# Attention, MLP and routed experts on one core: weights decoded through PSUM, page lists read early, one branch at the end

## The chip, the cores and the metric

The kernel runs on one core of a Trainium2 chip. The metric is the device time of one execution in microseconds: for the kernel before, the median of three runs is 1185.52 us (1181.2 to 1187.52). A core has five instruction queues that run side by side and wait for one another through semaphores: TensorE (matmuls and transposes), VectorE, ScalarE, GpSimd and SyncE, which only starts DMA transfers here.

## What is computed

Three stages, each the input of the next, all in fp32:

```python
# attention: 4 batches x 8 heads x 768 tokens x 64; the first 4 tokens and a window of 128 are visible
scores = np.where(is_sink | in_window, q @ k.T / 8, -1e9)
a = np.exp(scores - scores.max(-1)); a = a / (a.sum(-1) + 1e-09)
x = merge_heads(a @ v)                        # 3072 tokens x 512
# MLP1: 512 -> 2048 -> 512
h = x @ w_in;  x = (h - np.tanh(h)) @ w_out
# routed experts, one of 8 per token: 512 -> 1024 -> 512
logits = x @ w_gate + modality_bias[modality_id]
e = argmax(logits);  out[e == i] = gate * (relu(x[e == i] @ w1[i]) @ w2[i])
```

## The kernel before

**Tiling and stages.** The 3072 tokens are 12 chunks of 256. A chunk has 8 attention units (one head each, 96 in all, numbered U) and one pass through MLP1: 16 blocks f of the hidden width, each with 12 matmuls of the first layer (`L1`, line 175) and 6 of the second (`L2`, line 245). After a chunk, its tokens are routed: VectorE works out a slot for each token, and GpSimd scatters the tokens' numbers and gates to a table `xs` in DRAM (line 653). When all chunks are through, 13 expert pages of 256 tokens follow (functions `m_*`): SyncE loads the number of the page from `order`, reads the page's list `mpl` out of `xs` (line 740), VectorE turns it into two index lists (`mi`, `ms`), GpSimd gathers the tokens' rows with them (`mx`, line 750), and TensorE runs the expert's two layers. The expert's weights are loaded as `mr` (line 723) and split into a high part `mh` on ScalarE and a low part `ml` on VectorE. GpSimd scatters the results to `out` (line 801).

**fp32 on TensorE.** Most products are made from such high and low parts, three matmuls for one. A split is a cast (line 208 on ScalarE, 210 on VectorE) and a subtraction (line 213, on GpSimd or VectorE); both are helpers, so many tiles share these lines. The first 14 units (`nf=14`) are not split ("plain" units).

**An attention unit.** Scores `s` into PSUM (`a_S`); VectorE masks them and takes the row minimum (lines 316, 323); ScalarE takes the exponential and the row sum (line 325); GpSimd and VectorE make the reciprocal (328, 329); `a_norm` multiplies the 128x160 tile by it on GpSimd (line 334); TensorE transposes the result (`a_T`); GpSimd applies triangular masks (352); `a_PV` multiplies by v into the PSUM tile R, which ScalarE copies out for plain units.

**Weights of MLP1.** Each of the 32 blocks (16 of w_in, 16 of w_out, 512 KB) arrives as 8-byte numbers, two 32-bit words each. `w_decode` makes an fp32 number of the two words with three VectorE operations (lines 144, 146, 148) on the SBUF tile y, then ScalarE casts the high part and GpSimd subtracts. This happens once, beside the first chunk.

**PSUM.** `ps(kind, ...)` hands out banks: two each for three groups, r (scores and transposes), h (first layer) and R (R, and the transposes `x`). A group's tiles take its two banks in turn, so the third waits until the first has been read. Two more banks collect the second layer.

**Order.** `run_chunks` writes each step as an event with a due time from a table of numbers, sorts the events and emits them; a scheduler then sets the order of each engine's instructions, which are run strictly in that order. Slots for the first three pages (`EARLY`) are settled by `r_order(False)` before the last chunk is routed, so that their work can begin beside it. `r_redo` makes a flag that says whether the input needs a general version of the first stages; it is loaded by each engine and branched on (lines 940, 941). Another branch (lines 910, 915) runs further pages where more than 13 are needed. Neither is taken with these inputs. Line 998 is the end of the program.

Of the kernel before, what the change touches and what calls it, by code (L numbers as in the profile page):

```python
# [27 lines left out]
PG = 256  # L28
NPG = NT // PG + NE - 1
PADID = 4096.0  # L30
EARLY = 3
NSTAT = NT // PG + 1
# [8 lines left out]
class Kern:  # L41
    def __init__(self, tc, a):
        self.tc, self.nc, self.a = tc, tc.nc, a
        self.Wi, self.Wo = {}, {}
        self.o = dict(tc='a', xa='g', mt0=-0.28, gz='v', mxe=11, lx='v', nf=14, efh='a', trc=-14.17, tpf=-1.86, xhi='v', vhi='a', vlo='g', qhi='a', khi='v', sT='a', tr='a', ev='a', glo='g', whi='a', wlo='g', gk=0, wl=-8.54, wls=1.25, wd=-3.86, wds=1.05, wo=1, bs=2, be=3, bE=3, bV=1, bg=2, btr=1, bxt=1, pt={'h': 'h', 's': 'r', 'T': 'r', 'R': 'R', 'x': 'R', 'Q': 'R'}, pb=(('r', 2), ('h', 2), ('R', 2)), tl=-9.97, ts=-5.86, tv=-4.34, tsv=-2.34, tS=-5.24, dS=0.07, tN=-4, dN=0.5, tT=-1.78, dT=0.35, tPV=-0.39, txs=-0.28, tg=0.64, tre=0.05, trl=0.48, trr=3.39, u0=-15.64, g=2, lag=3.4, raw=2, sp=2, ghi='a', qlo='g', klo='v', eh='v', xlo='v', x2=4, me=13, mxl=8.77, mxt=1.5, mlag=1.45, mwl=9.99, mws=3.27, mm=0, ev0='v', ghi0='a', vhi0='a', sT0='a', qhi0='a', xlo0='g', eh0='v', y=2)

# [91 lines left out]
    def w_decode(self, f, which):  # L138
        nc = self.nc
        dic = self.Wi if which == "i" else self.Wo  # L140
        raw = dic[f]
        lo, hi = raw[:, :, 0], raw[:, :, 1]
        y = self.yp.tile([P, DM], I32, tag="y", name=f"y{which}{f}")
        nc.vector.tensor_scalar(out=y, in0=hi, scalar1=3, scalar2=0x3FFFFFF8,
                                op0=ALU.logical_shift_left, op1=ALU.bitwise_and)
        nc.vector.scalar_tensor_tensor(out=y, in0=lo, scalar=29, in1=y,
                                       op0=ALU.logical_shift_right, op1=ALU.bitwise_or)
        nc.vector.scalar_tensor_tensor(out=y, in0=hi, scalar=-0x40000000, in1=y,
                                       op0=ALU.bitwise_and, op1=ALU.bitwise_or)
# [181 lines left out]
    def a_norm(self, U, t):  # L331
        u = self.u[U]
        e, r = u["e"][t], u["sm"][:, t:t + 1]
        self.nc.gpsimd.tensor_scalar(out=e, in0=e, scalar1=r, scalar2=1.0, op0=ALU.mult, op1=ALU.mult)  # L334

# [364 lines left out]
    def r_redo(self, ok):  # L700

        nc = self.nc
# [10 lines left out]
        nc.vector.tensor_scalar(out=redo, in0=t, scalar1=-1.0, scalar2=1.0, op0=ALU.mult, op1=ALU.add)  # L713
        self.redo = redo


# [17 lines left out]

    def m_xload(self, g):
        nc = self.nc
# [7 lines left out]
        nc.vector.scalar_tensor_tensor(out=src, in0=pl[:, :, 1], scalar=float(NT), in1=pl[:, :, 1],  # L744
                                       op0=ALU.is_lt, op1=ALU.mult)
        self.mx[g] = []
        rows = NT - CH if g < EARLY else NT
        for t in range(n):
# [58 lines left out]
    def m_events(self, add, g, t, t0=-1e9):  # L807
# [3 lines left out]
        at(-o["me"], self.m_expert, g)  # L811
        at(-(o["mxe"] if g == 1 else o["mxl"]), self.m_xload, g)
        for j in range(PG // P):
# [14 lines left out]
    def run_chunks(self, banded):  # L828
# [3 lines left out]
        with ExitStack() as st:  # L832
# [70 lines left out]
            if banded:  # L903
                add(t2 + self.o["trr"] + .6, self.r_redo, self.ok)
            self.eg, self.mw, self.mx, self.mxt, self.mg, self.macc = {}, {}, {}, {}, {}, {}
# [3 lines left out]
            self.emit(ev)  # L909
            np_ = nc.values_load(self.npi[0:1, 0:1], min_val=0, max_val=NPG)  # L910

            def rest(g):
                if g == NPG:
                    return
                with tc.If(np_ > g):
                    ev.clear()
                    self.m_events(add, g, 0.0)
                    self.emit(ev)
                    rest(g + 1)

            rest(NSTAT)

def program(tc, a, o={}):
# [3 lines left out]
    with ExitStack() as st:  # L927
# [74 lines left out]
```

## Time and profile before

| | |
|---|---|
| median of three runs | 1185.52 us |
| the profiled execution | 1184.34 us |
| its span in the trace | 1182.6 us |
| TensorE busy | 1118.5 us, 95% of the span |
| VectorE busy | 860.0 us, 73% |
| ScalarE busy | 689.8 us, 58% |
| GpSimd busy | 636.3 us, 54% |

The profiled execution and its span differ by 1.7 us, which lie outside what the trace records. The shares are means over very different stretches: up to 150 us the first chunk's attention, the decode of the weights and the first chunk's MLP1 run beside each other; from there to about 815 us the chunks follow one another in a steady rhythm; from 815 to 890 us the last chunk, its routing and the first pages overlap; then come the pages, and from 1161 us on the last scatters and the branches. What a change is worth has to be read in its own stretch. A row of the timeline gives the start, the duration, the engine, the line and operation, and in brackets how long the engine stood idle before and what ended that.

### The profile page before, as it was taken

The numbers are of one execution on the slowest core, as the hardware profiler recorded it, in microseconds if no ns is written. First come the engines' busy times: TensorE is split into PE (matmuls) and PEld (weight loads), VectorE is DVE, ScalarE is ACT, GpSimd is POOL, SyncE is SP. The second block draws the span as 40 slices with busy tenths as digits, with TensorE's granted clock in tenths as the row PEclk, the third lists the DMA queues.
The fourth block names the chain that finished last, engine by engine and source line by source line (L and its number), as shares of the span: only waits on it lengthen the run. The fifth ranks groups of instructions, "written<-read, shape, count | busy, mean of one in ns | idle before, by whom it ended". The sixth has DMA issues, their size and how long they took to land. (4 is left out here: it accounts for less than half of the span.)

```text
span 1182.6 us, 22303 instructions
## 1 busy us (share of the span) xinstructions
PE 1118.5 (95%) x7171; PEld 984.5 (83%) x7171; DVE 860.0 (73%) x2227; ACT 689.8 (58%) x1643; POOL 636.3 (54%) x877
## 2 busy tenths in 40 slices
PE   7889989999999999999999999999889999999992
PEld 3346789998999999998999998998778899999992
DVE  6989878787887878797878888756757565666610
ACT  3345565766666666666776757654536555556620
POOL 4887766767676767676776767643223112111200
PEclk9989999999999999999999999999989999999997
DMA  6654222313132222222222322003629776777500
GB/s 203 211 181 145 69 71 61 91 50 98 55 83 61 66 81 68 86 63 74 68 86 62 92 52 85 27 24 107 267 79 353 219 221 220 243 215 215 162 18 6
DMA packets 75127, 137.14 MB, mean 116 GB/s; under 512 B 16241, under 2 KB 51313, under 8 KB 74993
## 3 DMA queue, kind: packets, MB, share of 16 engines
q1 hardware_dynamic: 70064, 122.40, 34.0%
q0 software_dynamic: 4928, 13.14, 3.1%
q8 instruction: 61, 1.00, 0.4%
q14 instruction: 74, 0.60, 0.2%
HBM read 122.86 MB, written 13.17 MB: 115 GB/s over the span
## 5 line engine op out<-in xcount | busy, mean ns | idle before, releaser
L175 PE MATMUL h<-xt,wi 128*128 128x256 f32 x2304 | 350.6, 291 | 6.0 <-DVE xt L210 3.0
L175 PEld LDWEIGHTS h<-xt,wi 128*128 128x128 f32 x2304 | 313.1, 193 | 30.1 <-DVE xt L210 5.8
L245 PE MATMUL acc<-wo,g 128*128 128x512 f32 x1152 | 313.6, 399 | 5.1 <-POOL g L213 3.5
L245 PEld LDWEIGHTS acc<-wo,g 128*128 128x128 f32 x1152 | 201.8, 189 | 38.2 <-POOL g L213 5.4
L732 DVE TENSOR_TENSOR ml<-mr,mh 128x1024 fp32r<-128x1024 f32 x104 | 129.8, 1257 | 52.8 <-ACT mh L731 51.0
L213 POOL TENSOR_TENSOR g<-gy,g 128x512 fp32r<-128x512 f32 x96 | 132.4, 1379 | 63.0 <-ACT g L208 60.3
L775 PE MATMUL mh<-mxt,mh 128*128 128x256 f32 x832 | 156.1, 284 | 0.9 <-ACT mxt L764 0.7
L792 PE MATMUL macc<-mh,mg 128*128 128x512 f32 x416 | 147.9, 401 | 4.4 <-DVE mg L779 4.3
L775 PEld LDWEIGHTS mh<-mxt,mh 128*128 128x128 f32 x832 | 136.9, 192 | 9.4 <-ACT mxt L764 0.9
L801 POOL DMA_INDIRECT out_dram<-mo,mi x26 | 29.3, 1128 | 196.7 <-ACT mo L800 192.5
L352 POOL TENSOR_SCALAR_AFFINE_SELECT X<-fl 128x512 fp32r<-128x512 f32 (+1 forms) x192 | 117.0, 633 | 30.7 <-DVE fl L382 22.0
L325 ACT ACTIVATE e<-e,nm 128x160 f32<-128x160 f32 x192 | 81.8, 426 | 87.6 <-DVE nm L323 71.1
L731 ACT CAST mh<-mr 128x1024 fp32r<-128x1024 f32 x104 | 108.2, 1051 | 38.6 <-PE macc L792 25.3
L775 PE MATMUL mh<-mxt,ml 128*128 128x256 f32 x416 | 117.6, 284 | 0.0
L190 ACT ACTIVATE u<-u,kt 128x512 f32<-128x512 f32 x96 | 69.5, 723 | 44.5 <-DVE h L189 23.3
L334 POOL TENSOR_SCALAR e<-e,sm 128x160 f32<-128x160 f32 x192 | 88.5, 472 | 9.7 <-DVE sm L329 8.0
L792 PEld LDWEIGHTS macc<-mh,mg 128*128 128x128 f32 x416 | 77.9, 190 | 18.1 <-DVE mg L779 5.3
L778 ACT ACTIVATE mg<-mh 128x256 fp32r<-128x256 f32 x104 | 40.1, 386 | 90.0 <-PE mh L775 85.9
L213 POOL TENSOR_TENSOR B<-q,A 128x256 fp32r<-128x256 f32 x82 | 71.5, 871 | 39.1 <-ACT A L208 38.2
L213 DVE TENSOR_TENSOR K<-k,K 64x448 fp32r<-64x448 f32 x82 | 85.1, 1038 | 2.7
L213 POOL TENSOR_TENSOR V<-v,V 128x256 fp32r<-128x256 f32 x82 | 65.0, 793 | 35.3 <-ACT V L208 35.2
L792 PE MATMUL macc<-ml,mg 128*128 128x512 f32 x208 | 82.4, 396 | 0.0
(211 smaller groups left out, 2200.2 us busy)
## 6 DMA issues: line engine op xcount, KB each, us to landing
mr<-in_moe_w_dram SPq DMA_DIRECT2D x104, 512.0 KB
k<-in_k_dram SPq DMA_DIRECT2D x82, 224.0 KB
v<-in_v_dram SPq DMA_DIRECT2D x96, 128.0 KB
q<-in_q_dram SPq DMA_DIRECT2D x82, 128.0 KB
rawi<-in_moe_w_in_dram SPq DMA_DIRECT2D x16, 512.0 KB
rawo<-in_moe_w_out_dram SPq DMA_DIRECT2D x16, 512.0 KB
x2d<-x SPq DMA_DIRECT2D x24, 256.0 KB
k<-in_k_dram SPq DMA_DIRECT2D x14, 112.0 KB
```

What stands on the lines that cost most here:

```text
L175: nc.tensor.matmul(h, w[:, wl, k * P:(k + 1) * P], x[:, xl, k], start=(n == 0), stop=(n == 11))
L190: nc.scalar.activation(u, u, AF.Relu, bias=self.kt, accum_out=self.over[:, n:n + 1])
L213: (self.nc.vector if eng == "v" else self.nc.gpsimd).tensor_tensor(out=out, in0=a, in1=b, op=ALU.subtract)
L245: nc.tensor.matmul(o, g[:, gl, q:q + P], w[:, wl], start=(f == 0 and n == 0), stop=(f == NF - 1 and n == 2))
L325: nc.scalar.activation(e, e, AF.Exp, bias=nm, scale=-1.0, accum_out=u["sm"][:, t:t + 1])
L334: self.nc.gpsimd.tensor_scalar(out=e, in0=e, scalar1=r, scalar2=1.0, op0=ALU.mult, op1=ALU.mult)
L352: self.nc.gpsimd.affine_select(out=out, in_=in_, pattern=[[0, n], [s, P]], base=0, channel_multiplier=-s, compare_op=ALU.is_gt if prev els ...
L731: nc.scalar.copy(hi, r)
L732: nc.vector.tensor_sub(lo, r, f32(hi))
L775: nc.tensor.matmul(h, w[:, k * P:(k + 1) * P], x[:, xl, k], start=(n == 0), stop=(n == 11))
L778: nc.scalar.activation(gt[:, 0], h, AF.Relu)
L792: nc.tensor.matmul(self.macc[g][t], gt[:, gl, t * P:(t + 1) * P], w[:, DM:], start=(f == 0 and n == 0), stop=(f == n8 - 1 and n == 2))
```

## The change

1. `w_decode`: the first two operations write the intermediate value z to a PSUM tile of the new kind 'y' in the group R, instead of to y in SBUF; the third reads z and writes y.
2. `a_norm`: for the 14 plain units the multiplication moves from GpSimd to ScalarE (an activation `Copy` with the reciprocal as scale).
3. The page's list gets a function of its own, `m_list` (the load of the page number, the list's DMA, the two VectorE operations). For the first three pages it is due right after `r_order(False)`; the gather stays with `m_xload`.
4. `r_redo` makes a second flag, `more` (two VectorE operations), which is set if either rare path is needed. The further pages move to `more_pages`, and one load and one branch guard both paths.

```diff
+        z = self.ps("y", I32, f"yp{which}{f}")
-        nc.vector.tensor_scalar(out=y, in0=hi, scalar1=3, scalar2=0x3FFFFFF8,
+        nc.vector.tensor_scalar(out=z, in0=hi, scalar1=3, scalar2=0x3FFFFFF8,
                                 op0=ALU.logical_shift_left, op1=ALU.bitwise_and)
-        nc.vector.scalar_tensor_tensor(out=y, in0=lo, scalar=29, in1=y,
+        nc.vector.scalar_tensor_tensor(out=z, in0=lo, scalar=29, in1=z,
                                        op0=ALU.logical_shift_right, op1=ALU.bitwise_or)
-        nc.vector.scalar_tensor_tensor(out=y, in0=hi, scalar=-0x40000000, in1=y,
+        nc.vector.scalar_tensor_tensor(out=y, in0=hi, scalar=-0x40000000, in1=z,
                                        op0=ALU.bitwise_and, op1=ALU.bitwise_or)
...
-        self.nc.gpsimd.tensor_scalar(out=e, in0=e, scalar1=r, scalar2=1.0, op0=ALU.mult, op1=ALU.mult)
+        if U < self.o["nf"]:
+            self.nc.scalar.activation(e, e, AF.Copy, scale=r)
+        else:
+            self.nc.gpsimd.tensor_scalar(out=e, in0=e, scalar1=r, scalar2=1.0, op0=ALU.mult, op1=ALU.mult)
...
+        nc.vector.scalar_tensor_tensor(out=t, in0=self.npg, scalar=float(NSTAT), in1=t, op0=ALU.is_le, op1=ALU.mult)
+        self.more = cp.tile([P, 1], I32, name="more")
+        nc.vector.tensor_scalar(out=self.more, in0=t, scalar1=-1.0, scalar2=1.0, op0=ALU.mult, op1=ALU.add)
...
-        at(-(o["mxe"] if g == 1 else o["mxl"]), self.m_xload, g)
+        x0 = o["mxe"] if g == 1 else o["mxl"]
+        if g < EARLY and t0 > 0:
+            add(t0, self.m_list, g)
+        else:
+            at(-x0 - .01, self.m_list, g)
+        at(-x0, self.m_xload, g)
...
-        redo = nc.values_load(K.redo[0:1, 0:1], min_val=0, max_val=1)
-        with tc.If(redo == 1):
-            K.general()
-            K.run_chunks(False)
+        more = nc.values_load(K.more[0:1, 0:1], min_val=0, max_val=1)
+        with tc.If(more == 1):
+            K.more_pages()
+            redo = nc.values_load(K.redo[0:1, 0:1], min_val=0, max_val=1)
+            with tc.If(redo == 1):
+                K.general()
+                K.run_chunks(False)
+                K.more_pages()
```

The change also moves instructions. VectorE's order where the decode of the weights begins, in the kernel before (L144, L146, L148 are a decode, L316 and L323 a unit's masks and minimum, `s_0_292` and its like the scores):

```order
58 L508 TENSOR_SCALAR moh<-idf 128x24
59 L510 TENSOR_TENSOR moh<-moh,moht 128x24
60 L509 TENSOR_SCALAR moht<-idf 128x24
61 L510 TENSOR_TENSOR moh<-moh,moht 128x24
62 L144 TENSOR_SCALAR yi_586<-rawi_480 128x512
63 L329 RECIPROCAL sm_252<-sm_252 128x2
64 L323 ISA e_0_296,nm_0_295<-s_0_292,mask_107 128x160
```

The same place in the changed kernel, where these lines are numbered one higher (`ypi` is the decode's tile in PSUM, L211 a cast of the MLP's input):

```order
89 L324 ISA e_0_516,nm_0_515<-s_0_512,mask_107 128x160
90 L324 ISA nm_0_515 128x1
91 L317 COPY_PREDICATED s_1_519<-mgt,s_1_519 128x128
92 L324 ISA e_1_523,nm_1_522<-s_1_519,mask_118 128x160
93 L324 ISA nm_1_522 128x1
94 L211 CAST xt_735<-xp_2_483 128x256
95 L145 TENSOR_SCALAR ypi_587<-rawi_480 128x512
```

The first decode operation stood behind the scores of unit 2 and stands behind those of unit 7 now.

GpSimd's order around the first gathers of rows, before (`g_3` to `g_7` are subtractions for the last chunk's MLP1, `xs` the scatters of routing, `mx` the gathers of pages 0, 1 and 2):

```order
722 L213 TENSOR_TENSOR g_3_11538<-gy_3_11532,g_3_11538 128x512
723 L213 TENSOR_TENSOR g_4_11589<-gy_4_11583,g_4_11589 128x512
724 L750 DMA mx_0_11509<-x2d,ms_11507 128x512
725 L750 DMA mx_1_11511<-x2d,ms_11507 128x512
726 L213 TENSOR_TENSOR g_5_11649<-gy_5_11643,g_5_11649 128x512
727 L750 DMA mx_0_11692<-x2d,ms_11690 128x512
728 L750 DMA mx_1_11694<-x2d,ms_11690 128x512
729 L213 TENSOR_TENSOR g_6_11727<-gy_6_11721,g_6_11727 128x512
730 L213 TENSOR_TENSOR g_7_11801<-gy_7_11795,g_7_11801 128x512
731 L653 DMA xs<-pl,sl_12094 4864x2 x2
732 L750 DMA mx_0_12193<-x2d,ms_12191 128x512
733 L750 DMA mx_1_12195<-x2d,ms_12191 128x512
```

And in the changed kernel:

```order
700 L214 TENSOR_TENSOR g_3_11600<-gy_3_11594,g_3_11600 128x512
701 L762 DMA mx_0_11571<-x2d,ms_11529 128x512
702 L762 DMA mx_1_11573<-x2d,ms_11529 128x512
703 L214 TENSOR_TENSOR g_4_11651<-gy_4_11645,g_4_11651 128x512
704 L762 DMA mx_0_11739<-x2d,ms_11546 128x512
705 L762 DMA mx_1_11741<-x2d,ms_11546 128x512
706 L214 TENSOR_TENSOR g_5_11711<-gy_5_11705,g_5_11711 128x512
707 L214 TENSOR_TENSOR g_6_11774<-gy_6_11768,g_6_11774 128x512
708 L214 TENSOR_TENSOR g_7_11848<-gy_7_11842,g_7_11848 128x512
709 L762 DMA mx_0_12228<-x2d,ms_11561 128x512
710 L762 DMA mx_1_12230<-x2d,ms_11561 128x512
711 L657 DMA xs<-pl,sl_12141 4864x2 x2
```

The gathers of pages 0 and 1 have each moved ahead of one subtraction, and those of page 2 ahead of the last chunk's scatters.

## Rows read from the trace of the kernel before

**Rows 1.** Stretches: length, then busy time of PE, PEld, DVE, ACT, POOL; PEclk.

```profile
20.00:149.00 129.00, 112.67 (x468) 72.25 (x468) 113.62 (x219) 64.18 (x168) 106.05 (x116) 0.95 0.51 166
149.00:815.00 666.00, 657.52 (x4549) 604.38 (x4548) 533.28 (x1626) 437.09 (x1177) 448.31 (x668) 0.99 0.24 67
```

**Rows 2.** Same view, DVE busy by the decodes' tiles yi, then yo.

```profile
20.00:149.00 129.00, 42.33 (x48) 0.95 0.51 166
20.00:149.00 129.00, 41.73 (x48) 0.95 0.51 166
```

**Rows 3.** Single lines, 20 to 149: ns min/median/max, first and last start, shapes.

```profile
L144 DVE TENSOR_SCALAR yi<-rawi x16: 414/422/1496, 20.4 to 127.2; 128x512 int32<-128x512 int32 x16
L146 DVE SCALAR_TENSOR_TENSOR yo<-rawo,yo x16: 678/693/1765, 22.9 to 134.0; 128x512 int32<-128x512 int32 x16
L189 DVE TENSOR_TENSOR h<-u,h x8: 683/684/690, 85.0 to 148.5; 128x512 f32<-128x512 f32 x8
L191 DVE SCALAR_TENSOR_TENSOR gy<-gy,h x7: 660/674/689, 86.1 to 142.9; 128x512 f32<-128x512 f32 x7
```

**Rows 4.** Groups of ACT and POOL, 20 to 149: busy us, mean ns | idle before.

```profile
L325 ACT ACTIVATE e<-e,nm 128x160 f32<-128x160 f32 x27 | 11.5, 425 | 11.9 <-DVE nm L323 8.3 <-POOL X L352 2.0 <-DVE sm L329 1.4
L208 ACT CAST wi<-yi 128x512 fp32r<-128x512 f32 x16 | 9.9, 618 | 19.0 <-DVE yi L148 18.8
...
L213 POOL TENSOR_TENSOR wi<-yi,wi 128x512 fp32r<-128x512 f32 x16 | 23.8, 1486 | 6.0 <-ACT wi L208 5.8
L334 POOL TENSOR_SCALAR e<-e,sm 128x160 f32<-128x160 f32 x28 | 20.7, 750 | 3.8 <-DVE sm L329 3.8
```

**Rows 5.** Timeline of PE, then DVE, in the first chunk.

```profile
11.80 2.39 PE L314 MATMUL s<-k,q 64*128 64x288 f32 x4
18.10 2.28 PE L314 MATMUL s<-k,q 64*128 64x288 f32 x4 [0.35 <-DVE nm L323]
...
82.47 1.32 PE L314 MATMUL s<-k,q 64*128 64x288 f32 x2
84.39 0.75 PE L314 MATMUL s<-k,q 64*128 64x288 f32 x2
...
20.39 0.43 DVE L144 TENSOR_SCALAR yi<-rawi 128x512 int32<-128x512 int32 x1 [1.47 <-DMA rawi<-in_moe_w_in_dram]
135.73 0.69 DVE L148 SCALAR_TENSOR_TENSOR yo<-rawo,yo 128x512 int32<-128x512 int32 x1
```

**Rows 6.** Timeline of PE at the change-over to pages.

```profile
838.51 3.44 PE L245 MATMUL acc<-wo,g 128*128 128x512 f32 x8 [3.12 <-POOL g L213]
...
880.79 1.22 PE L792 MATMUL macc<-mh,mg 128*128 128x512 f32 x2 [4.32 <-DVE mg L779]
881.81 0.63 PE L775 MATMUL mh<-mxt,mh 128*128 128x256 f32 x2
...
886.42 0.40 PE L775 MATMUL mh<-mxt,mh 128*128 128x256 f32 x2
...
889.78 0.63 PE L761 MATMUL mT<-ident,mx 128*128 128x128 f32 x4 [1.33 <-DMA mx<-x2d,ms]
```

**Rows 7.** Timeline there of POOL, SP (its DMA issues) and DVE.

```profile
817.34 1.29 POOL L213 TENSOR_TENSOR g<-gy,g 128x512 fp32r<-128x512 f32 x1 [3.24 <-ACT g L208]
...
870.73 1.02 POOL L653 DMA_INDIRECT xs<-pl,sl  x1 [27.70 <-DVE redo L713]
876.14 0.40 SPq L740 DMA_DIRECT2D mpl<-xs  x1
879.03 0.17 DVE L742 CAST mi<-mpl 128x2 int32<-128x2 f32 x1 [6.56 <-DMA mpl<-xs]
```

**Rows 8.** Single lines of POOL's queue at the end, columns as in rows 3.

```profile
L915 POOLq EVENT_SEMAPHORE  x4: 17/43/4642, 1163.5 to 1168.3; - x4
L915 POOLq INC_SWDGE_SEM  x1: 1699/1699/1699, 1168.4 to 1168.4; - x1
L998 POOLq DRAIN  x3: 40/107/6287, 1175.5 to 1182.3; - x3
```

More of the change, by code (lines that the diff above doesn't have):

```diff
@@ L44, in __init__ @@
         self.Wi, self.Wo = {}, {}
-        self.o = dict(tc='a', xa='g', mt0=-0.28, gz='v', mxe=11, lx='v', nf=14, efh='a', trc=-14.17, tpf=-1.86, xhi='v', vhi='a', vlo='g', qhi='a', khi='v', sT='a', tr='a', ev='a', glo='g', whi='a', wlo='g', gk=0, wl=-8.54, wls=1.25, wd=-3.86, wds=1.05, wo=1, bs=2, be=3, bE=3, bV=1, bg=2, btr=1, bxt=1, pt={'h': 'h', 's': 'r', 'T': 'r', 'R': 'R', 'x': 'R', 'Q': 'R'}, pb=(('r', 2), ('h', 2), ('R', 2)), tl=-9.97, ts=-5.86, tv=-4.34, tsv=-2.34, tS=-5.24, dS=0.07, tN=-4, dN=0.5, tT=-1.78, dT=0.35, tPV=-0.39, txs=-0.28, tg=0.64, tre=0.05, trl=0.48, trr=3.39, u0=-15.64, g=2, lag=3.4, raw=2, sp=2, ghi='a', qlo='g', klo='v', eh='v', xlo='v', x2=4, me=13, mxl=8.77, mxt=1.5, mlag=1.45, mwl=9.99, mws=3.27, mm=0, ev0='v', ghi0='a', vhi0='a', sT0='a', qhi0='a', xlo0='g', eh0='v', y=2)
+        self.o = dict(tc='a', xa='g', mt0=-0.28, gz='v', mxe=11, lx='v', nf=14, efh='a', trc=-14.17, tpf=-1.86, xhi='v', vhi='a', vlo='g', qhi='a', khi='v', sT='a', tr='a', ev='a', glo='g', whi='a', wlo='g', gk=0, wl=-8.54, wls=1.25, wd=-3.86, wds=1.05, wo=1, bs=2, be=3, bE=3, bV=1, bg=2, btr=1, bxt=1, pt={'h': 'h', 's': 'r', 'T': 'r', 'R': 'R', 'x': 'R', 'y': 'R'}, pb=(('r', 2), ('h', 2), ('R', 2)), tl=-9.97, ts=-5.86, tv=-4.34, tsv=-2.34, tS=-5.24, dS=0.07, tN=-4, dN=0.5, tT=-1.78, dT=0.35, tPV=-0.39, txs=-0.28, tg=0.64, tre=0.05, trl=0.48, trr=3.39, u0=-15.64, g=2, lag=3.4, raw=2, sp=2, ghi='a', qlo='g', klo='v', eh='v', xlo='v', x2=4, me=13, mxl=8.77, mxt=1.5, mlag=1.45, mwl=9.99, mws=3.27, mm=0, ev0='v', ghi0='a', vhi0='a', sT0='a', qhi0='a', xlo0='g', eh0='v', y=2)
     def e(self, k, start):
@@ L733, in m_wsplit, with m_list @@
         self.mw[g, f] = (hi, lo)
-    def m_xload(self, g):
+    def m_list(self, g):
         nc = self.nc
@@ L745, in m_xload @@
                                        op0=ALU.is_lt, op1=ALU.mult)
+        self.ml[g] = (pl, idx, src)
+    def m_xload(self, g):
+        nc = self.nc
+        pl, idx, src = self.ml[g]
         self.mx[g] = []
         rows = NT - CH if g < EARLY else NT
-        for t in range(n):
+        for t in range(PG // P):
             x = self.x2p.tile([P, DM], F32, tag="x2", name=f"mx{g}_{t}")
@@ L904, in run_chunks @@
                 add(t2 + self.o["trr"] + .6, self.r_redo, self.ok)
-            self.eg, self.mw, self.mx, self.mxt, self.mg, self.macc = {}, {}, {}, {}, {}, {}
+            self.eg, self.ml, self.mw, self.mx, self.mxt, self.mg, self.macc = {}, {}, {}, {}, {}, {}, {}
             for g in range(NSTAT):
@@ L909, in run_chunks, with more_pages @@
             self.emit(ev)
+    def more_pages(self):
+        tc, nc = self.tc, self.nc
+        with ExitStack() as st:
+            pool = lambda n, b, **k: st.enter_context(tc.tile_pool(name=n, bufs=b, **k))
+            self.xtp = pool("xt", self.o["bxt"])
+            self.gp = pool("g", self.o["bg"])
+            self.psr = pool("psr", 6, space=PSUM)
+            self.psa = pool("psa", 1, space=PSUM)
+            self.x2p = pool("x2", self.o["x2"])
+            self.rp = pool("rp", 1)
             np_ = nc.values_load(self.npi[0:1, 0:1], min_val=0, max_val=NPG)
@@ L915, in rest @@
                 with tc.If(np_ > g):
-                    ev.clear()
-                    self.m_events(add, g, 0.0)
+                    ev = []
+                    self.m_events(lambda t, fn, *a: ev.append((t, len(ev), fn, a)), g, 0.0)
                     self.emit(ev)
```

## The prediction, made before the changed kernel was run

> **What bounds the kernel now.** I read the busy times of each engine by stretches first, then the groups of VectorE and GpSimd in the stretch that is not TensorE's, then TensorE's timeline for every gap, and last the instructions behind the last matmul. From about 149 us to 815 us TensorE has hardly a gap, so nothing that this change touches there can shorten it; three places are left. The first is the start. In the 129 us from 20 to 149, VectorE is busy for 113.6 us and GpSimd for 106.1 us, 88% and 82% [rows 1]: these two run the stretch, and TensorE's first 82 us go at its lower level besides. The same pair of score matmuls takes 1.32 us at 82.47 and 0.75 us at 84.39 [rows 5]: 1.2 GHz, then 2.4 GHz, once matmuls of MLP1's first layer had run without a gap. The second place is the change-over from chunks to expert pages, with gaps of 3.12, 4.32 and 1.33 us on TensorE [rows 6]. The third is the end: from 1163.5 on GpSimd's queue works through branches, semaphores and a drain until the span ends at 1182.6 [rows 8].
>
> **Part 1, weights through PSUM.** The 32 weights cost VectorE 42.3 + 41.7 = 84.1 us [rows 2]. The last two operations of a decode have two levels: the second takes 0.68 us at best and up to 1.77 us [rows 3]. Two operations of the activation have the operands that the changed second and third will have (one SBUF input, one PSUM input, writing PSUM or SBUF, 128x512): they take 683 to 690 ns and 660 to 689 ns, in the same crowded stretch, with no upper level [rows 3]. So the second is 0.685 and the third 0.675. The first will read SBUF and write PSUM; no row has that. Its bounds are the 0.41 us that it takes at best now and the 0.69 us of the dearest PSUM row [rows 3]; I take 0.66, nearer to the rows that touch PSUM. A weight is then 2.02 us, 32 are 64.6 us, and VectorE's work falls by 19.5 us, from 113.6 to 94.1. The bounds of the first operation move that by 32 x 0.25 = 8 us down and 1 us up.
>
> The Trainium skill speaks against this part in "VectorE: DVE Perf Modes", section "Why PSUM operands drop a tier": an fp32 operand in PSUM keeps VectorE at its single rate, because PSUM gives it one read port. By that rule the first operation loses its 0.41 us, which is the value I took; were the rule not to reach a PSUM output, the stretch would be 8 us shorter in VectorE's work. No run here shows it yet.
>
> **What part 1 costs.** The scratch tile takes its turn in the two banks that the attention results (R) use, so a decode waits until the R two turns back has been read. The order shows the effect: before, the first decode stands behind unit 2's score reduction; after, behind unit 7's and behind the result of unit 5. It began at 20.39 and the last ended at 135.73 + 0.69 = 136.4 [rows 5], 3.63 us a weight. How late is it now? Without decodes beside them, units come every 18.10 - 11.80 = 6.30 us [rows 5], with TensorE busy throughout, at its lower level. Unit 7's scores then start at 11.8 + 5 x 6.3 = 43.3, unit 5's result ends 4.8 us later (scores 2.4, result 2.4), at 48.1, and with its copy out of the bank the first decode comes at 49, 29 us later than before.
>
> From there VectorE has the 94.1 us to do. (What it has done earlier, the scores of units 3 to 7, about 6 us, is made up by three more key splits that stand ahead of the same point in the new order.) Before, it was 88% busy; with GpSimd relieved and TensorE mostly ahead I take 92%: 49 + 102.3 = 151.3. Behind the last decode come a cast of 0.62 us, a subtraction of 1.49 us [rows 4] and 12 matmuls, some 3 us: 154. Before, that point was 149, but the new order has about 2 us more of TensorE's work done by then. **Start: +3 us.** Low bound: TensorE reaches its upper level early, the first decode comes at 41, VectorE is 97% busy: 41 + 97 + 3 - 2 = 139, -10. High bound: 85% busy: 49 + 110.7 + 3 - 2 = 160.7, +12.
>
> **Part 2, normalising on ScalarE.** GpSimd loses 28 operations of 750 ns, 20.7 us, and keeps 85 us in this stretch. ScalarE gains 28; the nearest row is its exponential of the same 128x160 tile, 425 ns, so 12 us [rows 4]. ScalarE is busy for 64 of the 129 us [rows 1], so this is free while it waits anyway (19 us of its idle time is waiting for decoded input weights alone). If the cover is gone, each of the 14 units' transposes waits behind one cast of 0.62 us, some 9 us in all; that is inside the high bound. The gain is inside the 92% and is not counted twice.
>
> **Part 3, lists ahead.** SyncE issues page 2's list only at 876.14, because its order load and the list stand behind the last chunk's scatters, which GpSimd issues at 870.73 after 27.7 us of waiting. VectorE sits idle 6.56 us for that list until 879.03, with a weight split and an activation queued behind it, and TensorE 4.32 us for that activation; then 1.33 us for the page's gathered rows [rows 6, 7]. After the 4.32 us gap its matmuls run at the lower level for some 5 us (two of one kind take 0.63 us at 881.81, 0.40 us at 886.42), which costs about 2.5 us. With the three lists read together near 817, all of this goes: -8.1 us. Next late there is a weight load, and those no longer stand behind the list either.
>
> The price: GpSimd's order now has page 0's two gathers ahead of g_4's subtraction, and page 1's ahead of g_5's. In the trace g_4's subtraction started at 817.34 [rows 7]. A list takes 2.9 us from its issue to VectorE's use of it (876.14 to 879.03), and two gathers about 1 us each like the scatter at 870.73, so with lists issued at 817 g_4 starts at about 822: 5 us later, of which TensorE may feel nothing or all. Against that page 1's gathers no longer stand ahead of g_6's subtraction, for which TensorE waits 3.12 us at 838.51 [rows 6]. I take these as even, between -3 and +5. **Change-over: -8 us, from -11 to -3.**
>
> **Part 4, one branch.** On GpSimd the first of the two branches waits 4.64 us for the last output scatters, until 1168.3 + 1.7 = 1170. Then come the load of redo, the second branch and its own semaphore steps. Only then, at 1175.5, does the final drain start, which takes 6.29 us [rows 8]. With one branch the drain starts at 1170.1: -5.4 us. It is less if the one branch, which now jumps over more code, has to wait for its target behind the scatters, which I bound by the 2.9 us that a small transfer takes [rows 7]: from -2.5 to -5.5. Two more VectorE operations of about 0.15 us stand near 870, where nobody waits for them. **End: -5.3 us.**
>
> **Sum.** 1184.3 + 3 - 8 - 5.3 = 1174.0 for the profiled execution. It lies 1.2 us below the median of 1185.5, so the forecast is 1175.
>
> **Rivals.** *The decode stays as slow as it was and only starts later.* If not VectorE's time but the two banks set the pace (a decode waits for an R, that R for scores that stand behind other decodes on the same VectorE), 3.63 us a weight stays, and the last ends at 49 + 32 x 3.63 = 165. With 3 us behind it and the 2 us of lead the start is +17; with the 12.6 us that lay between the last decode and 149 in the trace, +27. Take +22: 1174 + 19 + 1.2 = 1194, slower. Start at +13.3 is where it decides, a pace of 3.5 us a weight. For it: the late start is plain in the order. Against it: 0.7 us operations in place of those up to 1.77 us, and GpSimd's 20 us. *The start gains.* If TensorE gets to 2.4 GHz some 20 us earlier, because the first layer's matmuls now come in whole dozens soon after 50 instead of one or two at a time, or the first decode comes at 41: start -10, 1162. *The late parts give little:* the gap at g_4 stays in full and the branch waits for its code: change-over -3, end -2.5, 1182.
>
> **How the numbers follow.** The forecast (start -6 to +9, the rest about as above) has a chance of 0.52 and spans 1166 to 1181; the gain at the start 0.15, 1155 to 1166; the late parts giving little 0.16, 1179 to 1185; the slow decode 0.17, 1186 to 1200. About 0.5%, 6 us, is what a measurement of this kernel can tell from no change. Faster than 1179.6 are the second and most of the first: 0.60. Slower than 1191.4 is most of the last: 0.14. The rest is 0.26. For eight in ten the range runs from 1161 to 1190; it leaves out the lower half of the gain and the upper part of the slow decode.
>
> **What would show it.** In the changed kernel's trace: the second and third decode operations at 0.66 to 0.70 us without an upper level; the first at 0.6 or at 0.4; the first decode near 49; the end of the first chunk's first layer near 152; page 2's list at 817 and no gap near 880; perhaps a new gap near 821 that ends with g_4; the drain starting 6.6 us after the first branch's semaphore steps instead of 12. I am wrong if decodes still wait for banks, if TensorE stays at 1.2 GHz beyond 90 us, or if the drain waits for something other than the queue ahead of it.

## The result and the profile after

The changed kernel took 1167.89 us (median of four runs, 1165.2 to 1170.55) against 1186.26 us before; the ratio is 0.9861, 95% interval 0.9834 to 0.9888. The forecast was 1175 us, range 1161 to 1190. So the sign and the range held, and the gain was 18 us instead of 11. On another chip, later, the same kernel took 1168.89 us against 1183.29 us, ratio 0.9861 again (0.9837 to 0.9886).

The span of the profiled execution fell from 1182.6 to 1166.2 us. TensorE has the same 7171 matmuls in both, so its progress can be laid side by side. Three points split the span: the 2266th matmul (early in chunk 5, where both orders have done exactly the same matmuls), the first of expert page 3, and the end.

| | before | after | difference |
|---|---|---|---|
| 2266th matmul | 411.2 | 407.6 | -3.6 |
| from there to page 3 | 516.1 | 509.9 | -6.2 |
| from there to the end | 255.4 | 248.7 | -6.7 |

**The start.** First the stretch that answers to [rows 1], with its columns:

```profile
20.00:149.00 129.00, 114.82 (x485) 75.03 (x483) 96.41 (x231) 74.12 (x202) 73.47 (x98) 0.93 0.51 171
```

The three operations of a decode, which answer to [rows 3]:

```profile
L145 DVE TENSOR_SCALAR ypi<-rawi x16: 680/686/695, 48.4 to 140.6; 128x512 int32<-128x512 int32 x16
...
L147 DVE SCALAR_TENSOR_TENSOR ypo<-rawo,ypo x16: 668/689/697, 52.4 to 148.6; 128x512 int32<-128x512 int32 x16
...
L149 DVE SCALAR_TENSOR_TENSOR yo<-rawo,ypo x16: 672/677/689, 54.9 to 150.7; 128x512 int32<-128x512 int32 x16
```

VectorE's timeline at its first decode operation, as in [rows 5]:

```profile
48.40 0.69 DVE L145 TENSOR_SCALAR ypi<-rawi 128x512 int32<-128x512 int32 x1
```

VectorE's busy time in the 129 us fell from 113.6 to 96.4 us and GpSimd's from 106.1 to 73.5. The upper level of 1.77 us is gone without exception, and the first operation is up from 0.41 to 0.69 us. The first decode starts at 48.40, where 49 was worked out. The next view counts TensorE's instructions from the start up to the last matmul of chunk 0's first layer, and up to the common point; before comes first, then after (the columns are those of rows 1):

```profile
0.00:146.90 146.90, 124.26 (x486) 77.06 (x487) 120.83 (x273) 68.24 (x181) 111.06 (x149) 0.95 0.52 163
0.00:411.20 411.20, 382.78 (x2266) 315.29 (x2267) 334.65 (x921) 242.36 (x655) 293.20 (x423) 0.98 0.35 104
```

```profile
0.00:151.85 151.85, 130.58 (x530) 83.83 (x531) 108.97 (x301) 83.41 (x230) 81.57 (x134) 0.94 0.50 163
0.00:407.60 407.60, 381.18 (x2266) 314.89 (x2267) 320.37 (x921) 250.05 (x683) 255.69 (x395) 0.97 0.35 105
```

The first layer of chunk 0 ends 5 us later than before, but TensorE is 44 matmuls further by then, mostly attention of the next units. That lead is what counts: at the common point the changed kernel is 3.6 us ahead.

**The change-over.** TensorE's gaps there, then VectorE's wait for a list and SyncE's issues of the lists, all from the timeline, as in [rows 6, 7]:

```profile
822.40 0.95 PE L176 MATMUL h<-xt,wi 128*128 128x256 f32 x6 [0.84 <-DVE gy L192]
831.53 1.20 PE L246 MATMUL acc<-wo,g 128*128 128x512 f32 x4 [2.49 <-ACT g L209]
833.43 3.48 PE L246 MATMUL acc<-wo,g 128*128 128x512 f32 x8 [0.71 <-POOL g L214]
...
879.76 0.73 PE L804 MATMUL macc<-mh,mg 128*128 128x512 f32 x2 [2.45 <-DVE mg L791]
...
878.01 0.16 DVE L751 SCALAR_TENSOR_TENSOR ms<-mpl 128x2 int32<-128x2 f32 x1 [3.83 <-DMA mpl<-xs]
...
812.87 0.42 SPq L747 DMA_DIRECT2D mpl<-xs  x1
815.28 1.97 SPq L747 DMA_DIRECT2D mpl<-xs  x2
875.44 0.38 SPq L747 DMA_DIRECT2D mpl<-xs  x1
```

The three early lists are issued from 812.87 on, and the gaps of 4.32 and 1.33 us are gone. The gap of 3.12 us for GpSimd's subtraction has become 0.71, while the wait ahead of it for the same block's cast on ScalarE has grown from 1.42 to 2.49 us: 4.5 us together before, 3.2 after. And a gap of 2.45 us stands at 879.76: VectorE waits 3.83 us for a list again. This time it is page 3's, issued at 875.44, the first of those that are not read early.

**The end.** The single lines of GpSimd's queue, as in [rows 8]:

```profile
L971 POOLq EVENT_SEMAPHORE  x6: 17/30/931, 1155.9 to 1157.2; - x6
L971 POOLq COMPARE_BRANCH  x1: 53/53/53, 1153.1 to 1153.1; - x1
L971 POOLq INC_SWDGE_SEM  x1: 1708/1708/1708, 1157.3 to 1157.3; - x1
...
L1032 POOLq DRAIN  x3: 40/107/6287, 1159.1 to 1165.9; - x3
```

One branch, one set of semaphore steps, one step of 1.71 us, and the drain, which takes 6287 ns to the nanosecond as before. The last matmul ends 14.7 us before the end instead of 21.0.

### The profile page after: what moved, and what is told of

The parts are those of the page before. It is cut to its first block, busy times and chain, and to the rows that moved or that the text cites. A ratio compares the mean times of both kernels' runs of the same rounds, so it can differ in the third digit from the quotient of the medians.

```text
span 1166.2 us, 22233 instructions
## 1 busy us (share of the span) xinstructions
PE 1114.8 (96%) x7171; PEld 983.8 (84%) x7171; DVE 843.9 (72%) x2229; ACT 697.8 (60%) x1671; POOL 598.1 (51%) x849
## 4 chain that ended last, share of the span: by engine, by line
PE 76%; DVE 10%; issue 7%; POOL 3%; DMA 1%; ACT 0%; POOLq 0%; DVEq 0%; SPq 0%; ACTq 0%
PE h L176 19%; PE acc L246 18%; PE mh L787 11%; PE macc L804 10%; PE s L315 2%; PE s L312 2%; PE lg L579 2%; PE T L348 2%; PE R L418 2%; PE s L313 1%; DVE K L214 1%; PE T L349 1%; PE R L420 1%; PE R L406 1%; PE xT L572 1%
## 5 line engine op out<-in xcount | busy, mean ns | idle before, releaser
L804 PE MATMUL macc<-mh,mg 128*128 128x512 f32 x416 | 146.6, 398 | 2.5 <-DVE mg L791 2.5
L356 POOL TENSOR_SCALAR_AFFINE_SELECT X<-fl 128x512 fp32r<-128x512 f32 (+1 forms) x192 | 113.2, 612 | 38.7 <-DVE fl L386 23.5
L324 DVE CUSTOM_DVE_ANT_0 e<-s,mask 128x160 f32<-128x160 f32 x192 | 61.1, 318 | 35.6 <-PE T L349 26.0
L187 ACT ACTIVATE u<-h 128x512 f32<-128x512 f32 x96 | 56.5, 588 | 39.2 <-PE h L176 38.9
```

Of the source, the lines that this page charges most:

```text
L187: nc.scalar.activation(u, h, AF.Square)
L324: nc.vector.tensor_tensor_reduce(out=e, in0=s[:, P:QW], in1=self.mask[min(i, 2)], scale=-0.125, scalar=3.0e38, op0=ALU.add, op1=ALU.min, a ...
L356: self.nc.gpsimd.affine_select(out=out, in_=in_, pattern=[[0, n], [s, P]], base=0, channel_multiplier=-s, compare_op=ALU.is_gt if prev els ...
L804: nc.tensor.matmul(self.macc[g][t], gt[:, gl, t * P:(t + 1) * P], w[:, DM:], start=(f == 0 and n == 0), stop=(f == n8 - 1 and n == 2))
```

## Experiments

The table has each kernel with its median, the ratio to the kernel before on the same chip, and the three pieces of the span of its one profiled execution, from the start to the 2266th matmul, from there to page 3, and from there to the end. A kernel's runs scatter by some 5 us, and the pieces come from one run each, so a difference of 1 to 2 us in a piece means nothing; in the first piece the changed kernel's own two profiles differ by 3.9 us.

| kernel | median us | ratio (95%) | to 2266th | to page 3 | to the end |
|---|---|---|---|---|---|
| before | 1183.3 to 1186.3 | 1 | 411.2 | 516.1 | 255.4 |
| changed | 1167.9 | 0.986 (0.983 to 0.989) | 407.6 | 509.9 | 248.7 |
| changed, again | 1168.9 | 0.986 (0.984 to 0.989) | 411.5 | 510.4 | 249.1 |
| scratch in SBUF | 1165.7 | 0.984 (0.981 to 0.986) | 403.6 | 509.0 | 249.1 |
| normalised on GpSimd | 1165.1 | 0.983 (0.981 to 0.986) | 409.3 | 510.6 | 248.3 |
| both of these | 1173.0 | 0.991 (0.988 to 0.994) | 410.5 | 511.2 | 248.5 |
| scratch in SBUF, GpSimd busy | 1172.1 | 0.989 (0.988 to 0.991) | 409.5 | 511.7 | 248.8 |
| scratch in bank group h | 1164.4 | 0.983 (0.981 to 0.986) | 402.4 | 511.6 | 248.6 |
| the same, normalised on GpSimd | 1167.5 | 0.986 (0.983 to 0.988) | 401.6 | 511.4 | 248.8 |
| lists as before | 1178.1 | 0.993 (0.991 to 0.995) | 410.1 | 518.9 | 249.0 |
| two branches | 1174.6 | 0.992 (0.990 to 0.995) | 407.7 | 507.7 | 255.8 |
| page 3's list later | 1165.6 | 0.984 (0.981 to 0.986) | 407.8 | 508.0 | 248.4 |
| group h, page 3's list later | 1165.4 | 0.985 (0.983 to 0.988) | 404.6 | 510.6 | 248.4 |
| SBUF, page 3's list later | 1164.9 | 0.984 (0.982 to 0.986) | 403.2 | 508.3 | 248.6 |

**One part undone at a time.** The scratch first: z is y again, in SBUF.

```diff
-        z = self.ps("y", I32, f"yp{which}{f}")
-        nc.vector.tensor_scalar(out=z, in0=hi, scalar1=3, scalar2=0x3FFFFFF8,
+        nc.vector.tensor_scalar(out=y, in0=hi, scalar1=3, scalar2=0x3FFFFFF8,
...
```

> The changed kernel with the decode's scratch back in SBUF; the other three parts stay. The changed kernel took 1167.9 us against 1186.3 before; its trace puts 3.6 us of the 16.4 us of span at the start. Theory A (the scratch in PSUM pays for its late beginning and brings those 3.6 us): the long second and third decode operations of up to 1.77 us come back wherever GpSimd works beside them, the first decode goes back to about 20 us, and the time is 1170 to 1173 us. Theory B (the start is gained by GpSimd, which no longer normalises; the scratch in PSUM only makes the decode begin 28 us later): fewer long operations than before, an earlier start, 1161 to 1165 us, faster than the changed kernel.

Measured: 1165.7 us, no slower than the changed kernel, with the start at 403.6, 4 to 8 us ahead of the changed kernel's two profiles. Theory B came true in direction, 0.7 us above its range; of its signs the earlier start came, the fewer long operations did not. The stretch:

```profile
20.00:149.00 129.00, 113.09 (x501) 76.27 (x500) 119.15 (x225) 73.77 (x197) 89.58 (x94) 1.00 0.49 166
```

The costliest groups of the decode in it (busy us, mean ns, then idle time ahead), and the third operation before:

```profile
L148 DVE SCALAR_TENSOR_TENSOR yo<-rawo,yo 128x512 int32<-128x512 int32 x16 | 21.0, 1316 | 0.3
L148 DVE SCALAR_TENSOR_TENSOR yi<-rawi,yi 128x512 int32<-128x512 int32 x16 | 17.3, 1082 | 0.3
L146 DVE SCALAR_TENSOR_TENSOR yi<-rawi,yi 128x512 int32<-128x512 int32 x16 | 15.2, 948 | 0.3
```

```profile
L148 DVE SCALAR_TENSOR_TENSOR yo<-rawo,yo 128x512 int32<-128x512 int32 x16 | 17.7, 1105 | 0.3
L148 DVE SCALAR_TENSOR_TENSOR yi<-rawi,yi 128x512 int32<-128x512 int32 x16 | 14.6, 910 | 0.3
```

The long operations are not fewer: 29 second and third operations take over 0.85 us, against 25 before, and the third operation's mean is 1.1 to 1.3 us against 0.9 to 1.1. VectorE is busy for 119 of the 129 us, and yet the start is shorter. What changed beside it is GpSimd, at 89.6 us instead of 106.

The normalisation back on GpSimd:

```diff
-        if U < self.o["nf"]:
-            self.nc.scalar.activation(e, e, AF.Copy, scale=r)
-        else:
-            self.nc.gpsimd.tensor_scalar(out=e, in0=e, scalar1=r, scalar2=1.0, op0=ALU.mult, op1=ALU.mult)
+        self.nc.gpsimd.tensor_scalar(out=e, in0=e, scalar1=r, scalar2=1.0, op0=ALU.mult, op1=ALU.mult)
```

> The changed kernel with the normalisation of the first units back on GpSimd; the other three parts stay. Theory A (VectorE is the bound of the start; GpSimd has room once its subtractions are not slowed): the 28 operations are hidden, 1167 to 1170 us. Theory B (GpSimd's relief is what gains the start): 20 us of GpSimd's work come back into a stretch where it would be over 90% busy beside the late decode, 1173 to 1179 us. In both, decode operations stay near 0.69 us, as no operand pair in SBUF is left.

Measured: 1165.1 us, below the range of either theory; theory A's point, that GpSimd has room for the work, held. The work has also become smaller: with the scratch in PSUM a normalisation takes GpSimd 402 ns, where it took 750 before [rows 4]:

```profile
L335 POOL TENSOR_SCALAR e<-e,sm 128x160 f32<-128x160 f32 x31 | 12.1, 402 | 3.3 <-DVE sm L330 2.6 <-PE R L403 0.6
```

Its profiled execution was the slowest of its five, at 1169.9 us, so the piece of 409.3 says less than the median.

**Both undone.** As each part alone could be missed, the next question was whether either does anything. The edit is the two above together.

> The changed kernel without its two parts at the start: the decode's scratch in SBUF and the normalisation on GpSimd, as before; lists and branch as changed. Undone one at a time, each of these two parts left the time at 1165 us, no slower than with both. Theory A (they are substitutes: both lighten the same pair of engines, and one of them is enough): without either the start is as before, the late parts bring about 13 us, 1171 to 1174 us. Theory B (the start gains nothing from either; the 3.6 us in the trace come from elsewhere): 1165 to 1168 us.

Measured: 1173.0 us, theory A: the two are substitutes. By the ratios it is slower than either part alone, with no overlap of the intervals; its interval overlaps that of the changed kernel a little. With neither, the start is that of before (410.5 against 411.2), and the whole rest, 10 us in the median, comes from lists and branch.

**What ScalarE's normalising buys.** The scratch in SBUF, ScalarE normalising, and GpSimd given a multiplication that nobody needs:

```diff
             self.nc.scalar.activation(e, e, AF.Copy, scale=r)
+            self.nc.gpsimd.tensor_scalar(out=self.dummy, in0=self.dummy, scalar1=r, scalar2=1.0, op0=ALU.mult, op1=ALU.max)
```

> The changed kernel with the decode's scratch in SBUF, the normalisation on ScalarE, and in addition a GpSimd multiplication of the same 128x160 size into a tile that nobody reads, one beside each of the 28 normalisations, waiting for the same reciprocal. Without the additional operations it took 1165.7 us, without both parts at the start 1173.0 us. Theory A (what ScalarE's normalising buys is GpSimd's time): the time goes back to 1171 to 1174 us. Theory B (it buys a shorter chain from scores to transposes, since ScalarE does it in 0.42 us and GpSimd in 0.75 us): 1164 to 1168 us.

Measured: 1172.1 us, theory A: the gain is gone, although ScalarE's normalisation itself is as short as without the extra work (420 ns). The chain as a whole is not: from the start of a tile's exponential to the end of its normalisation a plain unit takes 7.34 us (mean of 28), against 6.56 us without the extra work and 7.36 us with both parts undone. GpSimd does the first step of the reciprocal that the normalisation waits for, and that step now queues behind the extra operations, so the loss of GpSimd's time acts through this chain and the two theories are not fully apart. The extra operations also cost more than those they stand for, 1182 ns against 750 in [rows 4], so the experiment overcharges GpSimd by some 10 us (24 of the 28 lie in the stretch, 28.4 us where 18 would have stood for them). GpSimd's total in the stretch is 112.6 us against 106.1 before:

```profile
20.00:149.00 129.00, 115.25 (x494) 76.26 (x493) 116.33 (x221) 72.94 (x193) 112.58 (x113) 0.88 0.52 166
```

The group of the additional operations:

```profile
L338 POOL TENSOR_SCALAR dummy<-dummy,sm 128x160 f32<-128x160 f32 x24 | 28.4, 1182 | 3.2 <-DVE sm L331 2.5
```

**Where the scratch lies.** The scratch takes turns with the first layer's tiles instead of the attention results:

```diff
- ... 'x': 'R', 'y': 'R'} ...
+ ... 'x': 'R', 'y': 'h'} ...
```

> The changed kernel with the decode's scratch in the two PSUM banks of the first MLP layer instead of the two of the attention results, so that in the order the first decode stands behind unit 2's scores again and not behind unit 7's. Theory A (the late beginning eats what the scratch in PSUM saves on VectorE): the first decode at 20 us with operations of 0.69 us, a start 5 us shorter or more, 1158 to 1164 us. Theory B (the start is bound by TensorE and by the chain through GpSimd and ScalarE, not by when the decode begins): 1165 to 1169 us.

Measured: 1164.4 us, just above theory A's range, against 1168.9 us of the changed kernel on the same chip; the two ratios' intervals still overlap (0.9808 to 0.9858 and 0.9837 to 0.9886). The start is 402.4 against 407.6 and 411.5. This kernel's first decode operation in the timeline:

```profile
20.31 0.69 DVE L145 TENSOR_SCALAR ypi<-rawi 128x512 int32<-128x512 int32 x1 [1.27 <-DMA rawi<-in_moe_w_in_dram]
```

And the stretch:

```profile
20.00:149.00 129.00, 113.11 (x508) 77.05 (x507) 101.86 (x250) 78.94 (x217) 79.99 (x109) 0.88 0.54 177
```

VectorE does more in the same stretch (101.9 us against 96.4) because its decodes have begun. This is theory A in direction: the late beginning eats some 5 us of what the scratch in PSUM saves. The edit also changes with whom the scratch shares its banks, but VectorE hardly waited for the banks in the changed kernel (0.9 us in all ahead of the 32 first operations). With this placement and GpSimd normalising:

> The changed kernel with the decode's scratch in the banks of the first MLP layer and the normalisation back on GpSimd. With the normalisation on ScalarE it took 1164.4 us. Theory A (either relief is enough, and the decode begins early here): 1164 to 1167 us. Theory B (GpSimd is the engine that bounds an early decode): 1169 to 1173 us, as without both parts.

Measured: 1167.5 us in the median, 0.5 us above theory A's range, with the start at 401.6, as good as any, in a profile that was the fastest of its five. Theory B's time is out: once the decode begins early with its scratch in PSUM, GpSimd can keep the normalisation. That does not clear GpSimd as the bound, because the scratch in PSUM has shortened GpSimd's own work, as the next rows show.

Over all fourteen profiles the 2266th matmul comes at 401.6 to 404.6 where the decode begins near 20 us and at least one of the two parts is there (five kernels), and at 407.6 to 411.5 in all others: where neither is there or GpSimd is kept busy (three, 409.5 to 411.2), and where the scratch shares the attention's banks (six).

**Whose relief counts?** These are the totals from the start to the 2266th matmul, where all kernels have done the same matmuls; VectorE's busy time is the third figure behind the length, GpSimd's the fifth. First the kernel with both parts undone and the one with GpSimd kept busy, which gain nothing; then the scratch in SBUF and the scratch in group h with GpSimd normalising, which gain 8 to 10 us:

```profile
0.00:410.50 410.50, 380.75 (x2266) 313.80 (x2267) 334.45 (x921) 242.28 (x654) 294.59 (x423) 0.96 0.35 104
0.00:409.50 409.50, 384.05 (x2266) 316.75 (x2267) 336.32 (x921) 251.42 (x682) 303.39 (x424) 0.95 0.35 104
```

```profile
0.00:403.65 403.65, 376.75 (x2266) 312.79 (x2267) 340.47 (x921) 249.59 (x683) 271.68 (x395) 1.00 0.35 106
0.00:401.60 401.60, 378.29 (x2266) 313.88 (x2267) 324.28 (x921) 242.21 (x655) 266.74 (x423) 0.97 0.35 106
```

GpSimd has 293 to 303 us of work in the three kernels that gain nothing (293.2 before) and 256 to 273 us in the other eleven, also where it keeps the normalisation. So each of the two parts takes 20 us or more from GpSimd. VectorE's time does not sort the kernels: with the scratch in SBUF it has 6 us more to do than before, and the start is 8 us shorter. The profiles therefore fit GpSimd alone as the engine whose relief counts. No run lightens VectorE and leaves GpSimd as it was, so whether VectorE's relief brings anything by itself is not shown.

**The lists.** Each list where its gather stands, as before:

```diff
-        if g < EARLY and t0 > 0:
-            add(t0, self.m_list, g)
-        else:
-            at(-x0 - .01, self.m_list, g)
+        at(-x0, self.m_list, g)
```

> The changed kernel with each page's list read where its gather stands, as before; the other three parts stay. Theory A (the trace's difference of 6.9 us between the last chunk and page 2 is this part alone): 1174 to 1176 us, TensorE's gaps of 3.1 and 4.3 us are back and that of 2.5 us before page 1's later matmuls, which waits behind page 3's list, is gone. Theory B (the wait only moved from page 2's list to page 3's, and the rest came from other timing): 1168 to 1171 us.

Measured: 1178.1 us, 9 to 10 us more than the changed kernel (8 by the ratios), above theory A's range. TensorE's two gaps are back, and VectorE's wait:

```profile
879.99 1.22 PE L804 MATMUL macc<-mh,mg 128*128 128x512 f32 x2 [4.51 <-DVE mg L791]
889.87 1.07 PE L773 MATMUL mT<-ident,mx 128*128 128x128 f32 x4 [2.80 <-DMA mx<-x2d,ms]
...
878.23 0.17 DVE L749 CAST mi<-mpl 128x2 int32<-128x2 f32 x1 [6.74 <-DMA mpl<-xs]
```

This part is worth 9.0 us in the piece to page 3 (518.9 against 509.9), the most of the four. Its worth depends on its company: without it the piece is 2.8 us longer than before, and with both parts at the start undone it is only 4.9 us shorter (511.2 against 516.1). Why is not shown. Then page 3's list, which the changed kernel still waits for, two blocks later:

```diff
-        x0 = o["mxe"] if g == 1 else o["mxl"]
+        x0 = o["mxe"] if g == 1 else o["mxl"] - 2.0 * (g == EARLY)
```

> The changed kernel with the list and gather of page 3 due two blocks later. In the changed kernel's trace VectorE waits 3.8 us for page 3's list and TensorE 2.45 us behind it at 880. Theory A (the list only stands too early in VectorE's and SyncE's queues): this gap goes, 2 to 4 us faster than the changed kernel, 1163 to 1166 us. Theory B (something else, such as the weights that are loaded late, is next): the gap only changes its releaser, 1167 to 1169 us.

Measured: 1165.6 us, in theory A's range and 3.3 us below the changed kernel's 1168.9 on that chip, intervals overlapping. The gap shrank and did not go, since VectorE still comes to the list too early:

```profile
882.44 0.73 PE L804 MATMUL macc<-mh,mg 128*128 128x512 f32 x2 [1.55 <-DVE mg L791]
...
881.82 0.17 DVE L749 CAST mi<-mpl 128x2 int32<-128x2 f32 x1 [2.73 <-DMA mpl<-xs]
```

**The branch.** The edit is the last block of the change, undone, with the further pages behind a branch of their own.

> The changed kernel with the two loads and two branches at its end as before; the other three parts stay. Theory A (GpSimd's queue is the chain to the end: a second load, branch and set of semaphore steps ahead of the drain): the drain starts some 11 us after the last scatter instead of 4.6, and the time is 1173 to 1175 us. Theory B (the drain waits for the scatters' landing and not for the queue ahead of it): 1167 to 1169 us.

Measured: 1174.6 us, and 7.1 us more in the last piece (255.8 against 248.7): theory A. The second load and the drain:

```profile
L971 POOLq TENSOR_LOAD <-redo x1: 306/306/306, 1158.5 to 1158.5; - x1
...
L1030 POOLq DRAIN  x3: 40/107/6287, 1164.1 to 1171.0; - x3
```

The drain follows the queue ahead of it and takes the same 6287 ns in every kernel.

**Combined.** Two attempts at a version that beats both, with page 3's list 3.2 blocks later and the scratch in group h, or in SBUF:

> The changed kernel with the decode's scratch in the banks of the first MLP layer and the list and gather of page 3 due 3.2 blocks later. Alone, the first gave 1164.4 us against 1168.9 of the changed kernel on that chip, the second (at 2 blocks) 1165.6. Theory A (they lie in different stretches and add): 1160 to 1162 us. Theory B (the start's gain is handed back later, or a smaller gap in front of page 2 only passes on): 1163 to 1166 us.

> The changed kernel with the decode's scratch in SBUF as before and the list and gather of page 3 due 3.2 blocks later. With the scratch in SBUF alone it took 1165.7 us. Theory A: 1162 to 1164 us, within 2 us of the version with the scratch in the first layer's banks: once ScalarE normalises, PSUM is not needed. Theory B (VectorE's two-level operations cost the start once the rest is out of the way): 1164 to 1167 us, slower than that version by 3 us or more.

Measured: 1165.4 and 1164.9 us. The first did not add (theory B): TensorE's gap for the list was still 1.89 us, and its piece to page 3 no shorter than the changed kernel's; the three kernels with group h have none below 510.6. The second lies 3 to 4 us below the changed kernel, above theory A's range, and within 1 us of the first, as theory A has it: once ScalarE normalises, the scratch need not lie in PSUM. The changed kernel again on the chip of three of these variants shows what such a difference is worth:

> The changed kernel itself, beside the others on one chip: 1166 to 1170 us, so that differences of 3 us between its variants can be judged.

Measured: 1168.9 us, and 1171.0 us of span in the profiled execution, with the start at 411.5. All variants at 1164 to 1166 us are faster than the changed kernel by less than 0.5%, which these runs cannot tell from no difference one by one.

## Why the prediction was right, and where it was off

**The start: +3 was forecast, -3.6 and +0.3 were seen** in the changed kernel's two profiles, and about -2 in the mean of the five that have both parts with the scratch in group R (408.9 against 410.9 for the two without either). Most steps as such held. The first decode came at 48.40, not 49. A weight's three operations take 2.05 us, not 2.02. The last decode ended at 151.4 and 154.3, where 151.3 was worked out, with VectorE busy 91% and 89% of the time, not 92%. The Trainium skill ("VectorE: DVE Perf Modes", section "Why PSUM operands drop a tier") says that any operand in PSUM caps VectorE's mode, at the single rate for fp32. The first operation's rise from 0.41 to 0.69 us agrees with that, although the section argues from read ports, and this operation only writes to PSUM, and in int32.

Two slips of the sum cancel, which is luck. It put 3 us between the last decode and the end of the first layer; there were 0.7 us, because the last weight decoded is one of w_out, and the last of w_in was decoded by 146.6. And it measured against 149, the edge of the stretch, where the first layer of the kernel before ended at 147.1. The end came at 152.1 and 154.9, so 4.9 and 7.8 us later than before, where the sum had 5.

The step that failed is the credit of 2 us for TensorE's work done by then: it is 44 matmuls, and at 0.148 us each, the rate from there to the common point ((411.2 - 146.9) / (2266 - 486)), that is an estimated 6.5 us. With that credit the step reads +3.3 - 4.5 = -1, inside what the profiles scatter. The profiles themselves give 4.9 + 3.6 = 8.5 and 7.8 - 0.3 = 7.5 us.

Beside it stands a term that the sum put at nothing. GpSimd was to lose the normalisations, 20.7 us, and to keep 85 us in the stretch. It had 73.5 us there, and 37.5 us less than before up to the common point (255.69 against 293.20), because its own operations became shorter with part 1. That this relief is what lets attention run 44 matmuls ahead fits the experiments, but is argued.

A second thing in this step was only partly right: that VectorE and GpSimd both run the stretch. The kernel with the scratch in SBUF has VectorE busier than before and a start 8 us shorter; the kernels without a gain are those in which GpSimd was not relieved. Taking 20 us from GpSimd in either way is enough, and the parts do not add. That the scratch's place in the two banks costs the late beginning was right, and it costs about 5 us. The rival of a decode that stays slow fell: the weights took from 48.4 to 151.4, 3.2 us each, below the 3.5 where it was to decide, and VectorE's idle time in front of all 32 first operations was 0.9 us.

The other rival, a start that gains by an earlier upper level of TensorE, came true in part, and in one profile of two. Up to 54.6 us the two profiles run alike. Then the score matmuls of one unit take 0.80 us in the first and 1.33 us in the second, the upper and the lower level by the pair in [rows 5]:

```profile
54.65 0.80 PE L315 MATMUL s<-k,q 64*128 64x288 f32 x2
```

```profile
54.63 1.33 PE L315 MATMUL s<-k,q 64*128 64x288 f32 x2
```

The second went on at the lower level until some time between 65 and 72 us and fell back to it once more around 88 us (granted clock 0.50 from 84 to 93). Of the six profiles with the scratch in group R, the three with the upper level by 56 us reach the common point at 407.6 to 407.8, the three with it later at 409.3 to 411.5. So most of the start's scatter goes with this; what decides it is not shown. It is not what gains the start elsewhere: with the scratch in SBUF the scores at 70.5 us still went at the lower level, and the start is 403.6. (The clock column of the stretches does not show this, as it reads 1.00 up to the first change that the trace records.) In the kernel before, the scores at 73.0 us went at the upper level for a moment, so not all of its first 82 us were at the lower one.

**The change-over: -8 forecast, -6.2 and -5.7 seen** in the piece to page 3. The gaps of 4.32 and 1.33 us went as written. The failed step is "next late there is a weight load": next late is the next page's list, by the same mechanism and at the same place, and takes 2.45 us back. TensorE did not pay the price at g_4: the lists came sooner than reckoned (VectorE used the first at 814.7), and g_4's subtraction started at 817.51. That is 3.4 us later against TensorE's own progress, which is 3.3 us ahead there, but no gap ends with it; the one of 0.84 us at 822.40 waits for VectorE. Undone in the company of the other parts, this part was worth 9 us.

**The end: -5.3 forecast, -6.3 and -5.9 seen** between last matmul and end. The mechanism is as described, and the branch that jumps over more code did not hold it up, because its 2.8 us until the queue goes on (1153.1 to 1155.9) run while the last scatters land. For the same reason the drain starts 3.2 us after the first semaphore step, not the 6.6 us of the forecast: the 4.64 us wait for the scatters [rows 8] has shrunk to 0.93 us behind the branch.

In sum, the forecast was 7 us too high. The sum of its terms was -10.3 us; the spans of the changed kernel's two profiles, 1166.2 and 1171.0 us, give -16.4 and -11.6. Up to 5 us of the error thus lies within what one execution differs from the next, 3.9 of it at the start.

## What to carry to other kernels

Undo each part of a change alone, and then together, before crediting it: here either part at the start could be left out, while leaving out both cost the whole gain of the start. Then add up each engine's time to a point where all variants have done the same work. It showed that two parts meant for two engines both relieved the same one. A scratch tile put into a rotating buffer inherits that buffer's order, so choose a buffer whose earlier turns are over when the scratch is wanted. When a wait is removed by reading something early, look at the first item that is not read early: it meets the same wait.

## What was not expected of the hardware

VectorE's operations on two SBUF tensors have their upper level beside GpSimd's work: of the 25 second and third operations of a decode that took over 0.85 us before, 22 overlap a GpSimd subtraction of two SBUF tensors; with one operand in PSUM none of 64 is long. An overlap alone is not enough: 15 of the other 39 have one too, of at most 0.67 us. GpSimd gains from it as well: its subtraction for a weight takes 1.31 us with the scratch in PSUM against 1.49 us [rows 4], its triangular masks 0.43 against 0.61. The masks before, then the three groups after:

```profile
L352 POOL TENSOR_SCALAR_AFFINE_SELECT X<-fl 128x256 f32<-128x256 f32 (+2 forms) x26 | 15.2, 606 | 0.5 <-ACT fl L208 0.4
```

```profile
L214 POOL TENSOR_TENSOR wo<-yo,wo 128x512 fp32r<-128x512 f32 x15 | 19.9, 1324 | 6.5 <-ACT wo L209 4.9 <-DMA v<-in_v_dram 1.6
L214 POOL TENSOR_TENSOR wi<-yi,wi 128x512 fp32r<-128x512 f32 x15 | 19.6, 1305 | 11.6 <-ACT wi L209 11.1 <-PE R L410 0.5
L356 POOL TENSOR_SCALAR_AFFINE_SELECT X<-fl 128x256 f32<-128x256 f32 (+2 forms) x28 | 11.4, 430 | 2.9 <-ACT fl L209 1.8 <-DVE fl L386 0.7
```

A GpSimd multiplication of 128x160 took 0.75 us with a multiplication by one as its second step and 1.18 us with a maximum as its second step, in the same crowded stretch. The two also work on different tiles, so that the second step is the reason is not shown.
